# Key copies of units 8 to 23: from VectorE and GpSimd copies to DMAs within SBUF

## The chip, the cores and the metric

The kernel runs on one core of a Trainium2 chip. The metric is the device time of one execution in microseconds (us). Names used below: PE is TensorE, DVE is VectorE, POOL is GpSimd, ACT is ScalarE, SP is SyncE, whose queue issues every DMA of this kernel. SBUF is the on-chip working memory, PSUM the memory that PE writes.

## The reference, cut to what matters

Three steps, all in float32 to high accuracy:

```python
# 1. banded attention with block summaries: q, k, v are [2, 8 heads, 768, 64], block 32, window 16
k_sum = k.reshape(B, H, nb, block, D).max(axis=3)      # "block maxima", 24 per head
v_sum = v.reshape(B, H, nb, block, D).mean(axis=3)
scores_all = concat([where(|i - j| < 16, scale * q @ k.T, -1e9), scale * q @ k_sum.T + log(32)])
attn = softmax(scores_all) @ concat([v, v_sum])
# 2. gated projection on x = attn as [1536, 512]; w_a, w_b are [512, 1536], w_out [1536, 512]
x = ((x @ w_a) * (x @ w_b)) @ w_out
# 3. second layer; w_in is [512, 2048], w_out [2048, 512]
h = x @ w_in;  out = (h - tanh(h)) @ w_out
```

## The kernel before, in words

**Attention in units.** The 2 x 768 positions are cut into 24 units of 64 positions. A unit sees at most 96 neighbouring keys (KW) and the 24 block maxima of its batch (NB), 120 columns in all (NK). The keys of a batch are transposed by PE and evacuated into one buffer `kt` (`prep_k`, L223 to L227): 768 columns of keys, then 24 of block maxima. `kt` has one buffer, so batch 1 (units 12 to 23) overwrites batch 0 (units 0 to 11) once all readers of batch 0 are done. For each unit, `W` (L281 to L289) copies the unit's 96 key columns and, where the buffer does not hold them yet, the 24 maxima from `kt` into a buffer of its own: units 8 to 11 have four of their own (tag "w"), units 12 to 23 take turns in two ("kw"). Then follow the scores (`T2m`, L295), the masked maximum (L306, DVE), the exponential (L310, ACT), the scaling (L324, ACT), a transpose (`T3`, L331) with its evacuation (L334), and the product with the values (`T4`, L344). T4's result x is kept as a rounded part (L351, ACT) and a residue (L352, DVE), since PE multiplies in a shorter format and each product is done as three: high x high, high x low, low x high.

**Blocks.** Eight units make a block of 512 positions. Units 0 to 7 run in the head, in an order written out by hand (`SEQ`, operations L614 to L771); their residues are L726. The units of the next block are spread between the projections of the block at hand.

**Projections.** Position after position PE runs `pos_a` (12 matmuls into PSUM bank "pa", L374), `pos_b` ("pb", L374) and, one group later, `pos_o` (12 matmuls, L402). a0, b0, o0 are those of the first column group, a1, b1 of the second. The result of a is evacuated by ACT (L382, tile ta), multiplied with that of b by DVE (L390, tile tg), and split again (L367 ACT, L368 DVE). The second layer follows with `pos_h` and `pos_o2` (L426, L463).

**Weights.** They come as 64-bit floats, in pieces of 512 KB (L141, L143, tiles stage, x21a, x21b). Piece 0 is for a0, 1 for b0, 2 for a1, 3 for b1, 4 for o0, and so on. A piece is decoded with two ACT steps (L154, L155), a clamp on POOL (L179) and three DVE steps (L161, L164, L165), and split by ACT (L184) and DVE or POOL (L185) into one of four buffers "wsp". Pieces 0 to 2 are done within `SEQ` (L750 to L771).

**What sets the order.** The head follows the order of the code on every engine. Behind it, up to position 72, SP's queue follows the order of the code while a scheduler with its own estimates orders PE, DVE, ACT and POOL; from position 72 on the order of the code holds everywhere. `W` is planned at its unit's place (L564, L565) and for units 8 to 11 in the head (L791, L792).

Of the kernel before, what the change touches and what calls it, by code (L numbers as in the profile page):

```python
# [16 lines left out]
ALU = mybir.AluOpType  # L17
# [22 lines left out]
def band_attention_moe_kernel(ctx: ExitStack, tc: tile.TileContext, q, k, v, w_a, w_b, w_out, w_in, w_out2, out):  # L40
    nc = tc.nc
    mm = nc.tensor.matmul

    B, H, S, D = q.shape
    NT, DM = out.shape
    BLK, WIN = 32, 16
    NB = S // BLK
# [7 lines left out]
    KW = 96  # L55
    NK = KW + NB
# [133 lines left out]
    kt, knat, qn, vst, qb, at_x, X = {}, {}, {}, {}, {}, {}, {}  # L190
# [7 lines left out]
    def kw_of(u):  # L198
        if 8 <= u < 12:
            if u not in kwx:  # L200
                kwx[u] = st([128, NP, NK], "w", 3 * F1)
            return kwx[u]
        return kwb[u % 4 if u < 8 else u % 2]
# [5 lines left out]
    def where(u):  # L209
        b, w = divmod(u, S // 64)  # L210
        return b, w, min(max(w * 64 - WIN, 0), S - KW)
# [37 lines left out]
    def load_q(m):  # L249
        b, w, _ = where(2 * m)  # L250
        t = st([128, H, D], "w", 3 * F1) if m < 8 else st([128, H, D], "qn", 3)
        nc.sync.dma_start(t, q[b, :, w * 64 : w * 64 + 128, :].rearrange("h p d -> p h d"))
        qn[m] = t

    def load_v(u):
        b, w, k0 = where(u)
        t = vw_of(u)
        nc.sync.dma_start(t[0:KW], v[b, :, k0 : k0 + KW, :].rearrange("h p d -> p h d"))
# [19 lines left out]
        for r in range(2):  # L278
            qb[2 * m + r] = qt[:, r]

    def W(u, eng):  # L281
        b, w, k0 = where(u)
        kw = kw_of(u)
        if eng is nc.gpsimd:
            eng.tensor_scalar(kw[:, :, 0:KW], kt[b][:, :, k0 : k0 + KW], 1.0, 0.0, op0=ALU.mult, op1=ALU.add)
        else:
            eng.tensor_copy(kw[:, :, 0:KW], kt[b][:, :, k0 : k0 + KW])
        if u < 4 or 8 <= u < 14:
            nc.vector.tensor_copy(kw[:, :, KW:NK], kt[b][:, :, S : S + NB])  # L289

    def T2m(u, tag):
        qt, kw = qb.pop(u), kw_of(u)
# [231 lines left out]
    def plan(j, fn, *args):  # L524
        at.setdefault(j, []).append((fn, args))
# [29 lines left out]
    for n, u in enumerate(range(8, 24)):  # L555
        j = (n - 8) * 4 + begin[1] + OFF if n >= 8 else n * (begin[1] // 8) + OFF
        b, w, _ = where(u)
        if u % 2 == 0:
            m = u // 2
            if m + 2 < 12:  # L560
                plan(j, load_q, m + 2)
            plan(j, T1, m, "pt", qbd)
            if u >= 12:
                plan(j, W, u, nc.vector)  # L564
                plan(j, W, u + 1, nc.vector)  # L565
        if u % 8 == 0:
            plan(j, new_x, u // 8)
        plan(j + 2, T2, u, "ps")
        plan(j + 3, T2b, u)
        plan(j + 5, T3, u, "pt")  # L570
        plan(j + 7, T4, u, "ps")
        if u + 3 < 24:
            plan(j + 7, load_v, u + 3)
            if 12 <= u + 3 < 15:
                plan(max(j + 7, VM + NC + 5), load_vm, u + 3)
# [6 lines left out]
    def run_plan(j):  # L582
        for fn, args in at.pop(j, ()):
            if fn in (T1, T2, T2b, T3, T4, W, prep_k) and HP:
                with tc.high_priority(offset=HP):
                    fn(*args)
            else:
                fn(*args)
# [199 lines left out]
    with tc.manual_schedule(engines=set(ET_HEAD)):  # L788
        load_q(4)
        load_v(8)  # L790
        for u in range(8, 12):  # L791
            W(u, nc.gpsimd if u % 2 else nc.vector)  # L792
        load_v(9)
        load_v(10)
        for j in range(-12, 0):
            run_plan(j)
# [41 lines left out]
```

## Time and profile before

| | us |
|---|---|
| median of three runs | 667.14 (666.83 to 668.13) |
| profiled execution | 668.39 |
| its span, first to last instruction | 666.6 |
| PE busy in the span | 645.6 |
| DVE busy | 509.3 |
| ACT busy | 471.9 |
| POOL busy | 208.1 |

The profile is of one execution. Its own time is 1.25 us above the median and 1.8 us above its span; differences worked out from its rows are differences of the span. An engine's busy time is the sum of its instructions, and the granted clock tells which share of full speed PE had: 1.00 is 2.4 GHz, 0.50 is 1.2 GHz.

### The profile page before, as it was taken

What the parts mean: (1) busy time and instruction counts of PE and PEld (TensorE: products, weight loads), DVE (VectorE), ACT (ScalarE), POOL (GpSimd) and SP (SyncE); (2) the same over time, 40 slices, a digit from 0 to 9 for tenths busy, and PEclk for the clock granted to TensorE, in tenths of its full rate; (3) what the DMA queues carried; (4) which work ended last, traced back from release to release, by engine and by line L of the source; (5) the groups of instructions that cost most, each with busy time, mean ns of one, the idle gap of its engine ahead of it and who ended that gap; (6) DMA issues with size and microseconds to landing.
All of it is one profiled execution on the core that took longest, in us unless ns stands there. A gap on an engine that the chain in (4) does not pass through costs nothing.

```text
span 666.6 us, 9629 instructions
## 1 busy us (share of the span) xinstructions
PE 645.6 (97%) x3240; PEld 520.3 (78%) x3240; DVE 509.3 (76%) x1019; ACT 471.9 (71%) x1002; POOL 208.1 (31%) x223
## 2 busy tenths in 40 slices
PE   7869999999899999999999999999999999999997
PEld 5658776888688888888888888888888888888885
DVE  5899998999766678637877748777777777777775
ACT  3878888788776778645655548777777777777774
POOL 5771122122001111000111134454444454444441
PEclk8989999999999999999999999999999999999999
DMA  9996996464415435413444200000010000010001
GB/s 205 246 204 202 214 225 184 152 187 132 129 55 168 151 107 167 131 48 111 142 143 142 80 1 0 1 0 1 0 64 1 0 1 0 24 40 1 1 0 63
DMA packets 84781, 62.11 MB, mean 93 GB/s; under 512 B 51892, under 2 KB 75444, under 8 KB 84732
## 3 DMA queue, kind: packets, MB, share of 16 engines
q1 hardware_dynamic: 84732, 61.50, 33.3%
q8 instruction: 25, 0.41, 0.2%
q14 instruction: 24, 0.20, 0.1%
HBM read 54.00 MB, written 7.34 MB: 92 GB/s over the span
## 4 chain that ended last, share of the span: by engine, by line
PE 84%; DVE 7%; ACT 3%; DMA 3%; issue 1%; SPq 1%; POOL 0%; DVEq 0%; ACTq 0%
PE acc L463 20%; PE pa L374 18%; PE pb L374 17%; PE acc L402 13%; PE pt L374 5%; PE ps L374 5%; PE ps L295 2%; PE ps L344 1%; PE pt L331 1%; DVE w L164 1%; PE pt L240 1%; DVE w L165 1%; DMA x20a<-in_q_dram 1%; SPq L614 1%; DMA w<-in_k_dram 1%
## 5 line engine op out<-in xcount | busy, mean ns | idle before, releaser
L185 POOL TENSOR_TENSOR wsp<-w,wsp 128x512 fp32r<-128x512 f32 x97 | 127.4, 1332 | 143.8 <-ACT wsp L184 143.8
L184 ACT ACTIVATE wsp<-w 128x512 fp32r<-128x512 f32 x201 | 121.3, 622 | 19.8 <-PE acc L402 10.1
L185 DVE TENSOR_TENSOR wsp<-w,wsp 128x512 fp32r<-128x512 f32 x104 | 74.7, 719 | 41.7 <-ACT wsp L184 41.5
L179 POOL TENSOR_SCALAR w<-w 128x512 f32<-128x512 f32 x52 | 39.5, 763 | 192.8 <-ACT w L154 184.0
L402 PE MATMUL acc<-gh,wsp 128*128 128x512 f32 x288 | 98.1, 400 | 0.0
L374 PE MATMUL pa<-XA,wsp 128*128 128x512 f32 x336 | 84.9, 399 | 4.6 <-DVE XA L726 4.6
L374 PE MATMUL pb<-XA,wsp 128*128 128x512 f32 x336 | 83.8, 395 | 0.9 <-ACT wsp L768 0.5
L463 PE MATMUL acc<-wsp,gh 128*128 128x512 f32 x256 | 80.5, 396 | 0.0
L374 PEld LDWEIGHTS pa<-XA,wsp 128*128 128x128 f32 x336 | 64.0, 191 | 18.7 <-ACT x21a L155 4.7
L374 PEld LDWEIGHTS pb<-XA,wsp 128*128 128x128 f32 x336 | 62.4, 189 | 15.2 <-ACT wsp L768 1.0
L367 ACT ACTIVATE gh<-tg 128x512 fp32r<-128x512 f32 x68 | 42.3, 622 | 30.6 <-DVE tg L390 30.2
L374 PE MATMUL pa<-XB,wsp 128*128 128x512 f32 x240 | 62.0, 402 | 1.4 <-ACT XB L351 1.4
L402 PEld LDWEIGHTS acc<-gh,wsp 128*128 128x128 f32 x288 | 53.4, 188 | 11.8
L374 PE MATMUL pb<-XB,wsp 128*128 128x512 f32 x240 | 60.0, 394 | 0.0
L402 PE MATMUL acc<-gl,wsp 128*128 128x512 f32 x144 | 56.9, 398 | 0.1
L463 PEld LDWEIGHTS acc<-wsp,gh 128*128 128x128 f32 x256 | 48.2, 188 | 11.1
L368 DVE TENSOR_TENSOR gl<-tg,gh 128x512 fp32r<-128x512 f32 x68 | 47.0, 691 | 9.4 <-ACT gh L367 9.3
L374 PEld LDWEIGHTS pa<-XB,wsp 128*128 128x128 f32 x240 | 45.2, 192 | 11.1 <-ACT XB L351 1.6
L374 PEld LDWEIGHTS pb<-XB,wsp 128*128 128x128 f32 x240 | 44.6, 188 | 9.7
L463 PE MATMUL acc<-wsp,gl 128*128 128x512 f32 x128 | 50.4, 394 | 0.0
L463 PE MATMUL acc<-wsp,vw 128*128 128x512 f32 x192 | 46.5, 390 | 0.0
L463 PEld LDWEIGHTS acc<-wsp,vw 128*128 128x128 f32 x192 | 35.9, 188 | 8.1 <-DVE vw L368 0.4
(305 smaller groups left out, 1184.0 us busy)
## 6 DMA issues: line engine op xcount, KB each, us to landing
stage<-in_moe_w_out_dram SPq DMA_DIRECT2D x19, 512.0 KB, 3.4
stage<-in_moe_w_in_dram SPq DMA_DIRECT2D x16, 512.0 KB, 5.2
stage<-in_moe_w_a_dram SPq DMA_DIRECT2D x8, 512.0 KB, 4.5
w<-wsc SPq DMA_DIRECT2D x16, 256.0 KB, 3.5
vw<-in_v_dram SPq DMA_DIRECT2D x19, 192.0 KB, 3.0
stage<-in_moe_w_b_dram SPq DMA_DIRECT2D x7, 512.0 KB, 5.0
wsc<-x21a SPq DMA_DIRECT2D x8, 256.0 KB, 4.8
wsc<-x21b SPq DMA_DIRECT2D x8, 256.0 KB, 5.9
```

The source lines that it names most:

```text
L164: nc.vector.scalar_tensor_tensor(r, t[:, :, 1], -0x40000000, r, op0=ALU.bitwise_and, op1=ALU.bitwise_or)
L165: nc.vector.tensor_tensor(r, r, t[:, :, 0], op=ALU.add)
L179: nc.gpsimd.tensor_scalar(rf, rf, HI_HI, HI_LO, op0=ALU.min, op1=ALU.max)
L184: nc.scalar.activation(s[:, 0, :], r, AF.Copy)
L185: eng.tensor_tensor(s[:, 1, :], r, s[:, 0, :].bitcast(F32), op=ALU.subtract)
L240: mm(pp, mavg[:, NB - 4 - 4 * c : 2 * NB - 4 - 4 * c], vch.pop(c).rearrange("p h d -> p (h d)"), start=(c == 0), stop=(c == NC - 1),)
L295: mm(pp[:, p, 0:NK], qt[:, p, :], kw[:, p, :], start=True, stop=True)
L367: nc.scalar.activation(dst[0], src, AF.Copy)
L368: eng.tensor_tensor(dst[1], src, dst[0].bitcast(F32), op=ALU.subtract)
L374: mm(dst, w, xx, start=(kk == 0 and n == 0), stop=(kk == KC - 1 and n == 2))
L402: mm(acc[blk][d][:, c0:c1], w, t, start=(f == 0 and c0 == 0 and n == 0), stop=(f == F1 - 1 and n == 2))
L463: mm(a[c], g[:, cs], s[:, i, :], start=(f == 0 and n == 0), stop=(f == F2 - 1 and n == 2))
```

## The change

`W` no longer takes an engine. The 96 key columns are copied by one DMA on SP's queue, and where the maxima are needed a second DMA copies 24 columns. The condition for the maxima is written as u < 14; `W` is called for units 8 to 23, so they are the same six units as before. Units 0 to 7 keep their copies in `SEQ`. There are 16 + 6 = 22 new DMAs in place of 14 DVE and 2 POOL copies of keys and 6 DVE copies of maxima. Lines of the changed kernel behind `W` have numbers lower by two; this text and the prediction name them by the numbers of before.

```diff
--- before.py
+++ after.py
@@ -278,15 +278,13 @@
         for r in range(2):
             qb[2 * m + r] = qt[:, r]
 
-    def W(u, eng):
+
+    def W(u):
         b, w, k0 = where(u)
         kw = kw_of(u)
-        if eng is nc.gpsimd:
-            eng.tensor_scalar(kw[:, :, 0:KW], kt[b][:, :, k0 : k0 + KW], 1.0, 0.0, op0=ALU.mult, op1=ALU.add)
-        else:
-            eng.tensor_copy(kw[:, :, 0:KW], kt[b][:, :, k0 : k0 + KW])
-        if u < 4 or 8 <= u < 14:
-            nc.vector.tensor_copy(kw[:, :, KW:NK], kt[b][:, :, S : S + NB])
+        nc.sync.dma_start(kw[:, :, 0:KW], kt[b][:, :, k0 : k0 + KW])
+        if u < 14:
+            nc.sync.dma_start(kw[:, :, KW:NK], kt[b][:, :, S : S + NB])
 
     def T2m(u, tag):
         qt, kw = qb.pop(u), kw_of(u)
@@ -561,8 +559,8 @@
                 plan(j, load_q, m + 2)
             plan(j, T1, m, "pt", qbd)
             if u >= 12:
-                plan(j, W, u, nc.vector)
-                plan(j, W, u + 1, nc.vector)
+                plan(j, W, u)
+                plan(j, W, u + 1)
         if u % 8 == 0:
             plan(j, new_x, u // 8)
         plan(j + 2, T2, u, "ps")
@@ -789,7 +787,7 @@
         load_q(4)
         load_v(8)
         for u in range(8, 12):
-            W(u, nc.gpsimd if u % 2 else nc.vector)
+            W(u)
         load_v(9)
         load_v(10)
         for j in range(-12, 0):
```

Three places where the order moves. First DVE, end of the head. Here XA is x of the first block, and `XA<-pa`, `XA<-pb` are the residues L726 of the two units computed last (1 and 3). Before:

```order
L726 TENSOR_TENSOR XA<-pt,XA 128x4x64
L287 COPY w<-kt 128x4x96
L289 COPY w<-kt 128x4x24 x2
L287 COPY w<-kt 128x4x96
L289 COPY w<-kt 128x4x24 x2
L726 TENSOR_TENSOR XA<-pa,XA 128x4x64
L759 TENSOR_SCALAR w<-w 128x512
L761 SCALAR_TENSOR_TENSOR w<-stage,w 128x512
L726 TENSOR_TENSOR XA<-pb,XA 128x4x64
```

In the changed kernel:

```order
L724 TENSOR_TENSOR XA<-pt,XA 128x4x64
L724 TENSOR_TENSOR XA<-pa,XA 128x4x64
L757 TENSOR_SCALAR w<-w 128x512
L759 SCALAR_TENSOR_TENSOR w<-stage,w 128x512
L724 TENSOR_TENSOR XA<-pb,XA 128x4x64
```

The six copies are gone, and the residue from "pa" stands directly behind the one from "pt".

A little later on DVE, in the changed kernel: the residue split of piece 2 (wsp), then the product for b0, and only then the three steps of decoding for piece 3 (x21a):

```order
L769 TENSOR_TENSOR wsp<-w,wsp 128x512
L388 TENSOR_TENSOR tg<-pb,ta 128x512
L277 COPY qbd<-pt 64x8x64
L161 TENSOR_SCALAR w<-w 128x512
L164 SCALAR_TENSOR_TENSOR w<-x21a,w 128x512
L366 TENSOR_TENSOR gl<-tg,gh 128x512
L165 ISA w<-x21a,w 128x1024
L161 TENSOR_SCALAR w<-w 128x512
```

Before, the decoding of piece 3 stood ahead of the product for b0. ACT shows the same. Here `x21a` is the load of piece 3, `x21b` of piece 4, and `ta<-pa` the evacuation of a0. Before:

```order
L768 ACTIVATE wsp<-w 128x512
L724 ACTIVATE XA<-pb 128x4x64
L752 ACTIVATE stage<-stage 128x512 x2
L154 ACTIVATE w<-x21a 128x512
L155 ACTIVATE x21a<-x21a 128x512
L768 ACTIVATE wsp<-w 128x512
L275 ACTIVATE qbd<-pt 64x8x64
L154 ACTIVATE w<-x21b 128x512
```

In the changed kernel:

```order
L766 ACTIVATE wsp<-w 128x512
L722 ACTIVATE XA<-pb 128x4x64
L750 ACTIVATE stage<-stage 128x512 x2
L766 ACTIVATE wsp<-w 128x512 x2
L155 ACTIVATE stage<-stage 128x512
L380 ACTIVATE ta<-pa 128x512
L154 ACTIVATE w<-x21a 128x512
L155 ACTIVATE x21a<-x21a 128x512
L275 ACTIVATE qbd<-pt 64x8x64
L154 ACTIVATE w<-x21b 128x512
L155 ACTIVATE x21b<-x21b 128x512
L155 ACTIVATE stage<-stage 128x512
```

The first step for piece 3 has moved from ahead of the evacuation of a0 to behind it.

Second SP, at the end of the head. The first row loads piece 5; `w<-kt` are the new copies of keys (96 columns) and maxima (24). Before:

```order
L141 DMA stage<-in_moe_w_a_dram 128x4x256
L258 DMA vw<-in_v_dram 96x8x64 x2
L214 DMA w<-in_k_dram 128x8x64
L252 DMA w<-in_q_dram 128x8x64
L141 DMA stage<-in_moe_w_b_dram 128x4x256
```

In the changed kernel:

```order
L141 DMA stage<-in_moe_w_a_dram 128x4x256
L285 DMA w<-kt 128x4x96
L287 DMA w<-kt 128x4x24
L285 DMA w<-kt 128x4x96
L141 DMA stage<-in_moe_w_b_dram 128x4x256
L287 DMA w<-kt 128x4x24
L285 DMA w<-kt 128x4x96
L143 DMA stage<-in_moe_w_out_dram 128x1024
L287 DMA w<-kt 128x4x24
L285 DMA w<-kt 128x4x96
L287 DMA w<-kt 128x4x24
L258 DMA vw<-in_v_dram 96x8x64 x2
```

The loads of pieces 6 and 7 (w_b and w_out) now stand among the copies, and the loads of v, k and q behind them.

Third PE, at the end of the first block. XB is x of the second block; `pt<-ident,qn` are the transposes of q for unit 16, `ps<-at,vw` is T4 of unit 15, `ps<-kw` the scores of units 16 and 17. Before:

```order
L402 MATMUL acc_886<-gl,wsp 128x512
L402 MATMUL acc_886<-gh,wsp 128x512
L269 MATMUL pt<-ident,qn 128x128 x4
L344 MATMUL ps<-at,vw 64x64 x8
L374 MATMUL pa<-XB,wsp 128x512
L374 MATMUL pb<-XB,wsp 128x512
L295 MATMUL ps<-kw,qbd 128x120 x4
L374 MATMUL pa<-XB,wsp 128x512 x11
L374 MATMUL pb<-XB,wsp 128x512 x11
```

In the changed kernel:

```order
L400 MATMUL acc_886<-gh,wsp 128x512
L329 MATMUL pt<-ident,e 120x128 x4
L342 MATMUL ps<-at,vw 64x64 x8
L269 MATMUL pt<-ident,qn 128x128 x4
L372 MATMUL pa<-XB,wsp 128x512
L372 MATMUL pb<-XB,wsp 128x512
L372 MATMUL pa<-XB,wsp 128x512 x11
L372 MATMUL pb<-XB,wsp 128x512 x11
L293 MATMUL ps<-kw,qbd 128x120 x4
```

Before, eight L402 stood between the transposes of unit 15 (L331) and these rows; they now stand ahead of those transposes. The transposes of q have moved behind T4, and the scores of unit 16 from ahead of the long run on "pa" to behind that on "pb".

## Rows read from the trace of the kernel before

**Rows 1.** The page's busy times: engine, us, share of the span, instructions.

```profile
PE 645.6 (97%) x3240; PEld 520.3 (78%) x3240; DVE 509.3 (76%) x1019; ACT 471.9 (71%) x1002; POOL 208.1 (31%) x223
```

**Rows 2.** Stretches of the span: us; busy us and instructions per engine; granted clock; DMA share; GB/s.

```profile
44.00:48.00 4.00, 3.45 (x9) 2.38 (x10) 3.79 (x8) 1.91 (x4) 1.31 (x2) 0.50 1.37 210
48.00:60.00 12.00, 12.00 (x55) 9.88 (x55) 11.53 (x28) 9.88 (x26) 2.53 (x4) 0.90 0.74 212
60.00:80.00 20.00, 19.61 (x115) 15.90 (x114) 18.49 (x41) 16.90 (x41) 3.82 (x5) 1.00 0.78 202
80.00:100.00 20.00, 19.46 (x110) 15.74 (x109) 19.50 (x42) 16.31 (x39) 5.53 (x7) 1.00 1.00 229
...
300.00:400.00 100.00, 100.00 (x438) 81.88 (x437) 72.47 (x113) 55.52 (x98) 16.53 (x19) 1.00 0.30 103
```

**Rows 3.** Chain of waits, 34 to 66 us: start, us, engine, tile, line.

```profile
41.81 1.79 DVE w L289 x2
```

**Rows 4.** Order of time on DVE, 36 to 62 us: start, us, line, operation, tiles.

```profile
39.95 0.41 DVE L726 TENSOR_TENSOR XA<-pt,XA 128x256 fp32r<-128x256 f32 x1
40.29 0.40 DVE L287 COPY w<-kt 128x384 f32<-128x384 f32 x1
40.61 0.62 DVE L289 COPY w<-kt 128x96 f32<-128x96 f32 x2
41.15 0.66 DVE L287 COPY w<-kt 128x384 f32<-128x384 f32 x1
41.73 1.87 DVE L289 COPY w<-kt 128x96 f32<-128x96 f32 x2
43.53 0.41 DVE L726 TENSOR_TENSOR XA<-pa,XA 128x256 fp32r<-128x256 f32 x1
...
45.38 0.68 DVE L763 CUSTOM_DVE_ANT_0 w<-stage,w 128x1024 uint16<-128x1024 uint16 x1
```

**Rows 5.** Order of time on PE, 30 to 95 us; in brackets the wait ahead.

```profile
44.08 0.77 PE L374 MATMUL pa<-XA,wsp 128*128 128x512 f32 x1 [4.58 <-DVE XA L726]
...
47.79 3.68 PE L374 MATMUL pa<-XA,wsp 128*128 128x512 f32 x10
...
57.69 2.88 PE L374 MATMUL pb<-XA,wsp 128*128 128x512 f32 x12
```

**Rows 6.** Order of time on ScalarE, 36 to 62 us.

```profile
42.42 0.65 ACT L154 ACTIVATE w<-x21a 128x512 f32<-128x512 f32 x1
```

**Rows 7.** Groups of instructions: count, busy us, mean ns, idle before.

```profile
L390 DVE TENSOR_TENSOR tg<-pb,ta 128x512 f32<-128x512 f32 x36 | 24.6, 684 | 10.1 <-PE pb L374 9.8
...
L306 DVE CUSTOM_DVE_ANT_0 e<-ps,mask 128x120 f32<-128x120 f32 x64 | 14.1, 274 | 5.2 <-PE ps L295 5.2
```

**Rows 8.** DMA issues: tiles, queue, count, KB each, median us to landing.

```profile
vw<-in_v_dram SPq DMA_DIRECT2D x19, 192.0 KB, 3.0
...
w<-in_q_dram SPq DMA_DIRECT2D x4, 256.0 KB, 6.0
```

**Rows 9.** Half-microsecond stretches with 1 KB pieces, then with 256-byte pieces on the queue.

```profile
42.50:43.00 0.50, 0.00 (x0) 0.00 (x0) 0.50 (x1) 0.50 (x3) 0.50 (x1) 1.00 1.06 369
...
45.00:45.50 0.50, 0.50 (x4) 0.30 (x2) 0.50 (x3) 0.00 (x0) 0.00 (x0) 0.50 1.40 197
```

**Rows 10.** Order of time on SP's queue, 0 to 320 us.

```profile
40.50 0.37 SPq L141 DMA_DIRECT2D stage<-in_moe_w_a_dram  x1
...
141.83 0.33 SPq L258 DMA_DIRECT2D vw<-in_v_dram  x1
```

**Rows 11.** Order of time on PE, 95 to 160 us: scores of unit 14.

```profile
150.68 1.05 PE L295 MATMUL ps<-kw,qbd 128*128 128x120 f32 x8
```

**Rows 12.** Chain of waits, 165 to 190 us.

```profile
171.76 4.08 DMA stage<-in_moe_w_in_dram
```

**Rows 13.** Order of time on PE, 160 to 230 us: the second block's first matmul.

```profile
178.34 0.50 PE L374 MATMUL pa<-XB,wsp 128*128 128x512 f32 x1 [1.43 <-ACT XB L351]
```

## The prediction

> **What bounds the kernel now.** I read the page's busy times first. TensorE (PE) is busy for 645.6 of 666.6 us [rows 1], so the kernel can gain at most the 21 us in which PE rests, plus what PE loses at a low clock. The table by stretches shows where that is: from 300 to 400 us PE runs 438 matmuls in 100 us, 0.23 us each, with nothing left over, while from 44 to 48 us the granted clock is 0.50, the 1.2 GHz level, and from 48 to 60 us still 0.90 in the mean [rows 2]. So PE bounds nearly everything, and the open stretch is the change from the head (attention of units 0 to 7) to the first projection, about 39.5 to 60 us. The chain of waits goes through VectorE (DVE) there: 1.79 us of it is the copy of the block maxima [rows 3]. The order of time on DVE shows why. Between the residue of one unit, which ends at 40.36, and that of the next, which starts at 43.53, stand two copies of keys and four of block maxima for units 8 to 11 [rows 4]. PE's first projection matmul waits 4.58 us for exactly that residue (XA by L726): it needs the PSUM bank "pa", which the residue still reads [rows 5]. After 60 us PE is full, and DVE too: 18.49 and 19.50 of 20 us busy in the two stretches to 100 us [rows 2]. DVE's finishing times matter that long, later they have slack.
>
> **The copies in the head.** DVE loses six copies that fill 40.29 to 43.53, 3.24 us [rows 4]. The order shows the residue for "pa" directly behind the one for "pt". So the residues, the last decoding steps of pieces 1 and 2 and the start of projection a0 all move forward by 3.24 us; GpSimd, which loses two key copies, is no later. The ten matmuls of a0 that ran from 47.79 [rows 5] can start at 47.79 - 3.24 = 44.55.
>
> What is late next is weight piece 3, for projection b1. Before, ScalarE took up its first step at 42.42 [rows 6]. In the changed order that step stands behind the evacuation of a0, and DVE's three steps for it stand behind the product for b0 (L390), which needs b0 finished on PE. At full clock a0's ten end at 44.55 + 2.3 = 46.85 and b0's ten, next in PE's order, at 49.15. Then DVE has before the residue split of piece 3: L390, L277, three decoding steps, L368, L161, four score maxima, L164 and the split. By the 0.68 of a 512-wide step, 0.42 of a shift (as the short residue) and 4 x 0.27 for the maxima [rows 4, 7] that is 7 x 0.68 + 2 x 0.42 + 1.1 = 6.7, less some 0.5 by which records overlap: 6.2 us. The split ends at 55.35, and b1's third matmul, the first that reads it, starts near 55.5. Before, b1 began at 57.69 [rows 5] and its third matmul came 0.47 later, 58.2. That is 2.7 us earlier, less 0.4 for four key transposes that PE had done by then and now does later: **+2.3 us** as the upper bound.
>
> The lower bound is the clock. Before, half clock lasted to about 50.4 (0.10 below full over 12 us is 2.4 us at half [rows 2]). If it lasts as long now, 44.55 to 50.4 at half speed costs 2.9 us: b0 ends at 52.05, b1's third matmul starts at 58.4, and the term is -0.6 us. PE rests less ahead of a0 than before (two short waits in place of one of 4.58 us), but it is still little used from 39.5 to 44. I expect half clock for about half of those 5.85 us, which costs 1.45 us and leaves 2.3 - 1.45, and take **+0.9 us**. That DVE stays full to 100 us, and so may take back some of what PE is ahead, is a reason not to take more.
>
> **The new DMAs.** 22 DMAs are added on SP's queue: 16 of keys (196,608 bytes in 512 pieces of 384 bytes) and 6 of maxima (49,152 bytes in 512 pieces of 96). No row shows this form from SBUF to SBUF. The nearest are v loads of 192 KB, which land 3.0 us after issue in the median, and q loads of 256 KB in a full queue, 6.0 [rows 8]; I take those as both ends for one copy, and 3 to 4 once the queue is short. For the queue's own time the row of the 1 KB pieces moves 369 GB/s and that of the 256-byte pieces 197 GB/s [rows 9]. 197 GB/s is 770 pieces per us, so 512 pieces hold the queue 0.67 us; by bytes alone a key copy would be 0.53. I take 0.67 for each DMA.
> In the head SP issues the load of piece 5 at 40.50 [rows 10], then three key copies and two of maxima mixed with the loads of pieces 6 and 7. Piece 7 then lands near 40.9 + 1.4 + 5 x 0.67 + 2 x 1.4 + 1.5 = 50 (1.4 is 512 KB at 369 GB/s, 1.5 what remains of a landing). ScalarE comes to it only behind work that ends near 51 to 52, so the loads are covered, with 1 to 2 us to spare: **0**, if the price per DMA holds.
> From unit 12 on the copies are issued behind a v load that waits for PE's output matmuls of an earlier unit. For unit 14: v load at 141.83 [rows 10], one weight load, one q load and two key copies at about 0.5 us each, so the second is out at 144 and lands at 147 to 150, against 150.68 for the scores in the old order [rows 11]. The cover is 0.7 to 3.7 us, so **0**. What is queued behind on SP are weight loads and stores for the last layer; they go out 1 us later, and the engine that waits for them is ScalarE.
>
> The Trainium skill, "DMA: Bandwidth & Descriptors", Specifications, says that transfers under 512 bytes are slower since the DMA engine reads and writes back. By it every added piece would cost more than the row of the 256-byte loads. The same page, "Why small descriptors are slow (HBM only)", says that SBUF to SBUF does not suffer from small pieces; by that 0.53 would do. The trace agrees that 256-byte pieces from HBM move at about half the rate [rows 9]; it holds no pieces of this size within SBUF.
>
> **DVE from 57 us on.** Ten of the twelve later key copies, at 0.40 us or less [rows 4], lie where PE is full; freeing them is worth nothing beyond the cover it gives to the first two.
>
> **The block boundary.** At 178.34 the second block's first matmul waited 1.43 us, and ScalarE got there late because it had waited for a weight load of 4.08 us [rows 12, 13]. The scheduler reorders PE there: the block's L402 now all stand ahead of the transposes of unit 15, which leaves T4 of that unit without cover (about 1.5 us more waiting), but the transposes of q now cover the wait behind T4, and the scores of unit 16 come one pair of projections later. I bound this by -1.5 and +2.0 us (the wait of 1.43 gone and little clock lost) and take **+0.5**: one pair's worth of work (0.23 x 2) in place of the wait.
>
> **Sum.** 0.9 + 0 + 0 + 0.5 = 1.4 us less. The profiled execution took 668.39 us (666.6 of span and 1.8 around it), which gives 667.0; it is 1.25 above the median of 667.14. The measured median should go to 667.14 - 1.4 = **665.7 us**.
>
> **Rivals.**
> Given back (no change): the order that keeps piece 3 behind b0 and the half clock use up the whole start. For it: DVE idles some 3 us for b0 in the new order and has almost no room until 100 us [rows 2]. Against it: the split of piece 3 still comes out earlier by the sum at full clock. Time: 667.14 with the -0.6 to +0.6 of that term, 666.5 to 667.7.
> Slow small copies (slower): if one DMA of 512 small pieces holds the queue 2.0 us, not 0.67, the five ahead of piece 7 take 10 us, it lands at 56.6 (50 + 5 x 1.33), ScalarE holds the split of piece 3 until then, and b1 begins 4.8 us later than forecast: 4.8 - 1.4 = 3.4 us slower, 670.5. It eats the gain from about 1.35 us per DMA on (1.8 us of slack and 1.4 of gain, over five). For it: nothing of this form is in the trace, and 256-byte pieces are already at half rate [rows 9]; against it: 192 KB in 768 pieces land in 3.0 us in all [rows 8]. The skill's rule on transfers under 512 bytes would point this way.
> Clock stays up (more): the shorter rests ahead of a0 leave PE at 2.4 GHz, the first term is +2.3 and the boundary gains its 2.0: 662.8.
>
> **How the numbers follow.** Forecast 0.48 (its own range 664 to 667), given back 0.27, slow copies 0.14, clock stays up 0.11. About 0.2%, 1.33 us, can be told from no change here. The forecast case lies beyond that in 0.39 of its 0.48 (a stall shorter than reckoned adds to it more easily than a longer one takes), the clock case fully: faster 0.50. Given back and the rest of the forecast, less 0.04 for a new wait that no row points to: same 0.32; slower 0.18. The range runs from the clock case to the start of the slow case: 662.5 to 668.6.
>
> **What would show it.** Right: PE's first projection matmul near 40.9 and a0's ten near 44.6; a wait of PE in b1 for a split by L185 near 53 to 55.5; the key copies landing within 3 to 4 us and no wait of PE's score matmuls on a DMA. Wrong: a0 still at 44 (the copies were not the cause); ScalarE waiting over 2 us for pieces 6 or 7 (slow copies); half clock past 50 us, which takes the first term; or PE waiting in scores of units 12 to 23 for kw.

## The result and the profile after

The changed kernel takes 671.43 us (median of 4 runs, 670.69 to 673.34), against 667.14 before: ratio 1.0064 [1.0051, 1.0078]. It is slower by 4.3 us where 1.4 us less were forecast. Its profiled execution took 671.29 us with a span of 669.6, which is 3.0 more than the span of before; the rest of the 4.3 lies in the profiled execution of before, 1.25 above its median.

The page's busy times (engine, us, share, instructions) answer to [rows 1]:

```profile
PE 646.5 (97%) x3240; PEld 520.9 (78%) x3240; DVE 501.8 (75%) x999; ACT 473.1 (71%) x1002; POOL 206.1 (31%) x221
```

VectorE lost 20 instructions and 7.5 us, and the span still grew. The stretches answer to [rows 2] (us; busy us and instructions of PE, weight loads, DVE, ACT and POOL; granted clock; DMA share; GB/s):

```profile
44.00:48.00 4.00, 4.00 (x11) 3.15 (x10) 2.58 (x3) 1.21 (x2) 1.46 (x1) 0.50 1.04 258
48.00:60.00 12.00, 9.48 (x41) 7.48 (x40) 8.42 (x23) 9.56 (x24) 2.28 (x3) 0.93 0.84 199
60.00:80.00 20.00, 20.00 (x112) 16.48 (x112) 18.61 (x40) 15.87 (x37) 4.51 (x6) 0.96 0.78 209
80.00:100.00 20.00, 19.01 (x109) 15.22 (x108) 18.58 (x40) 17.95 (x43) 5.96 (x8) 1.00 1.09 256
...
300.00:400.00 100.00, 100.00 (x439) 81.93 (x438) 71.38 (x111) 54.23 (x96) 16.52 (x19) 1.00 0.32 103
```

From 48 to 60 us TensorE now rests for 2.5 of 12 us where it was full before, and the clock is below full again from 60 to 80. From 300 us on TensorE is full at full clock in both. TensorE's rows (order of time; the wait in brackets) answer to [rows 5, 13]; L711 is the last T4 of the head, L400 the first output product:

```profile
38.05 0.67 PE L711 MATMUL pb<-gh,w 120*64 120x64 f32 x16
40.66 0.49 PE L372 MATMUL pa<-XA,wsp 128*128 128x512 f32 x1 [1.95 <-DVE w L757]
42.73 0.79 PE L372 MATMUL pa<-XA,wsp 128*128 128x512 f32 x1 [1.58 <-DVE XA L724]
...
45.03 3.87 PE L372 MATMUL pa<-XA,wsp 128*128 128x512 f32 x10
48.74 2.43 PE L372 MATMUL pb<-XA,wsp 128*128 128x512 f32 x10
...
55.80 0.73 PE L372 MATMUL pb<-XA,wsp 128*128 128x512 f32 x2 [1.03 <-ACT wsp L184]
58.03 4.14 PE L372 MATMUL pb<-XA,wsp 128*128 128x512 f32 x10 [1.49 <-DVE wsp L185]
...
62.36 0.48 PE L400 MATMUL acc<-gh,wsp 128*128 128x512 f32 x1
...
181.00 1.01 PE L342 MATMUL ps<-at,vw 120*64 120x64 f32 x16 [2.00 <-ACT at L332]
```

The same two points in the kernel before:

```profile
38.84 0.67 PE L713 MATMUL pb<-gh,w 120*64 120x64 f32 x16
...
60.41 0.39 PE L402 MATMUL acc<-gh,wsp 128*128 128x512 f32 x1
```

The first projection matmul came at 40.66, 3.42 us earlier than before. But 0.79 us of that stood already at the last T4 of the head, ahead of the place where the copies had been, and is not the change's: in the fourteen profiles of this document that T4 starts anywhere from 37.98 us (late_p3_behind) to 39.30 (late_copies), and neither of these two has a new transfer. Then b1 waited twice, 2.52 us together, for its own weights (piece 3), and its last ten took 4.14 us, against 2.43 for b0's ten at full clock, since the clock had fallen a second time. The first output product came at 62.36, 1.95 us later than before; counted from the last T4 of the head it is 2.74 us later. ScalarE and VectorE show why b1's weights were late; they answer to [rows 6] and [rows 4]:

```profile
48.94 0.60 ACT L380 ACTIVATE ta<-pa 128x512 f32<-128x512 f32 x1 [1.66 <-PE pa L372]
49.43 0.66 ACT L154 ACTIVATE w<-x21a 128x512 f32<-128x512 f32 x1
```

```profile
51.27 0.69 DVE L388 TENSOR_TENSOR tg<-pb,ta 128x512 f32<-128x512 f32 x1 [3.86 <-PE pb L372]
...
54.40 0.69 DVE L165 CUSTOM_DVE_ANT_0 w<-x21a,w 128x1024 uint16<-128x1024 uint16 x1
...
56.88 1.10 DVE L185 TENSOR_TENSOR wsp<-w,wsp 128x512 fp32r<-128x512 f32 x1
```

ScalarE took up piece 3 at 49.43, not at 42.42, behind an evacuation that itself waited for TensorE; VectorE idled 3.86 us for b0's product with piece 3's steps queued behind it. The copies themselves, as transfers (tiles, queue, count, KB, median us to landing; answer to [rows 8]):

```profile
kw<-kt SPq DMA_DIRECT2D x12, 192.0 KB, 4.2
...
w<-kt SPq DMA_DIRECT2D x4, 192.0 KB, 4.3
w<-kt SPq DMA_DIRECT2D x4, 48.0 KB, 4.4
```

They land some 4 us after issue in the median, and no row of TensorE waits for one of them.

For all kernels below I use one measure of where time goes: from a table of half-microsecond stretches, TensorE's resting time plus its busy time times (1 - granted clock), added up over the head, the middle of block 0, and the boundaries of blocks 1 and 2. It comes from the one profiled execution of each, and so is rough: a_late_head and tail_on_top have the same order in the head, and yet the granted clock from 40 to 50 us is 0.83 in one profile and 0.66 in the other, and the head columns are 5.8 and 6.8. Differences of about 1 us in a column may be the execution and not the kernel. The ratios rest on all runs; the kernels ran beside runs of the kernel before, on several chips.

| kernel | ratio to before [95%] | 36-62 us | 62-176 us | 176-302 us |
|---|---|---|---|---|
| before | 1 | 8.1 | 1.0 | 3.6 |
| changed | 1.0064 [1.0051, 1.0078] | 10.6 | 2.3 | 3.7 |
| head_dma | 1.0040 [1.0028, 1.0053] | 9.8 | 2.4 | 2.1 |
| tail_dma | 1.0009 [0.9995, 1.0023] | 8.1 | 1.5 | 2.2 |
| dma_on_top | 1.0031 [1.0018, 1.0044] | 8.8 | 2.4 | 2.2 |
| p3_early | 1.0070 [1.0048, 1.0091] | 7.6 | 2.2 | 5.3 |
| p34_head_dma | 1.0047 [1.0029, 1.0065] | 6.9 | 4.1 | 3.7 |
| p34_after | 1.0031 [1.0019, 1.0043] | 6.0 | 4.8 | 1.7 |
| late_copies | 0.9997 [0.9983, 1.0010] | 5.2 | 2.2 | 1.5 |
| a_late | 1.0037 [1.0022, 1.0051] | 6.2 | 2.5 | 2.1 |
| a_late_head | 1.0003 [0.9992, 1.0014] | 5.8 | 3.2 | 1.1 |
| tail_pool | 0.9995 [0.9984, 1.0006] | 5.9 | 1.6 | 2.3 |
| tail_on_top | 0.9975 [0.9963, 0.9987] | 6.8 | 3.2 | 1.3 |
| late_p3_behind | 0.9960 [0.9944, 0.9975] | 7.8 | 1.3 | 0.2 |

By this measure the changed kernel loses 2.5 us more than before in the head, 1.3 from 62 to 176 us and 0.1 at the boundaries. The first matmul of block 2 tells the same in time: it starts at 298.73 for 295.69, 3.04 us later, and this lag stays to the end. Of it 1.95 stood at the first output product; the other 1.1 arose between there and block 2.

### The profile page after: what moved, and what is told of

The parts are those of the page before. It is cut to its first block, busy times and chain, and to the rows that moved or that the text cites. A ratio compares the mean times of both kernels' runs of the same rounds, so it can differ in the third digit from the quotient of the medians.

```text
span 669.6 us, 9637 instructions
## 1 busy us (share of the span) xinstructions
PE 646.5 (97%) x3240; PEld 520.9 (78%) x3240; DVE 501.8 (75%) x999; ACT 473.1 (71%) x1002; POOL 206.1 (31%) x221
## 4 chain that ended last, share of the span: by engine, by line
PE 80%; DVE 8%; DMA 5%; ACT 3%; issue 1%; SPq 1%; POOL 0%; DVEq 0%
PE acc L461 20%; PE pa L372 17%; PE pb L372 17%; PE acc L400 12%; PE pt L372 5%; PE ps L372 5%; PE ps L293 1%; DMA w<-in_k_dram 1%; DVE w L164 1%; DVE w L165 1%; PE ps L342 1%; DMA stage<-in_moe_w_in_dram 1%; DMA x21b<-in_moe_w_a_dram 1%; PE pt L240 1%; DMA x20a<-in_q_dram 1%
## 5 line engine op out<-in xcount | busy, mean ns | idle before, releaser
L400 PE MATMUL acc<-gh,wsp 128*128 128x512 f32 x288 | 98.2, 400 | 1.1 <-ACT wsp L184 1.1
L372 PE MATMUL pb<-XA,wsp 128*128 128x512 f32 x336 | 85.5, 401 | 3.3 <-DVE wsp L185 2.2
L400 PEld LDWEIGHTS acc<-gh,wsp 128*128 128x128 f32 x288 | 53.7, 188 | 13.5 <-ACT wsp L184 1.7
L400 PE MATMUL acc<-gl,wsp 128*128 128x512 f32 x144 | 56.9, 398 | 0.0
```

The costliest lines, as they stand in the source:

```text
L372: mm(dst, w, xx, start=(kk == 0 and n == 0), stop=(kk == KC - 1 and n == 2))
L400: mm(acc[blk][d][:, c0:c1], w, t, start=(f == 0 and c0 == 0 and n == 0), stop=(f == F1 - 1 and n == 2))
```

## The experiments

Theory T: the loss is in the order of the instructions, above all in the place of piece 3's decode. Theory D: the transfers cost it. Theory L: the later units cost it. The code hands its operations to the scheduler in numbered plan slots: slot j is emitted just ahead of position j of the projections, and the slots below 0 at the end of the head, where the order on SP, ACT, DVE and POOL is still fixed. Diffs show only the lines that matter.

**One half of the change at a time.** head_dma:

```diff
         kw = kw_of(u)
+        if u < 12:
+            nc.sync.dma_start(kw[:, :, 0:KW], kt[b][:, :, k0 : k0 + KW])
+            if u < 14:
+                nc.sync.dma_start(kw[:, :, KW:NK], kt[b][:, :, S : S + NB])
+            return
```

> Units 8 to 11 by DMA as in the changed kernel, units 12 to 23 copied on VectorE as before. Theory T (the loss is in the order of the instructions: with the six head copies gone, ScalarE takes piece 3's decode behind a0's evacuation and VectorE takes it behind b0's product, so TensorE waits for b1's weights and its clock falls a second time): the first o product of block 0 starts near 62.4 us as in the changed kernel (60.4 before), the total is 668.5 to 670.5. Theory D (the transfers cost the time, about 4.3 us for 22 of them): 8 of 22 are left, so about 668.7 and nothing is bound to the wait for b1's weights. Theory L (the 14 later transfers and the order behind 60 us cost it): 666.5 to 667.8.

670.41 us (before, beside it, 667.86). The head is that of the changed kernel:

```profile
57.28 4.63 PE L379 MATMUL pb<-XA,wsp 128*128 128x512 f32 x10 [1.49 <-DVE wsp L185]
62.42 0.78 PE L407 MATMUL acc<-gh,wsp 128*128 128x512 f32 x1
```

tail_dma has the same lines under `if u >= 12:`.

> Units 8 to 11 copied by VectorE and GpSimd as before, units 12 to 23 by DMA. Theory T: head as before, the first o product at 60.4 +- 0.3 us, and the total 667.1 to 668.5 (what the changed order behind 60 us costs, up to 1.3). Theory D: 14 of 22 transfers, so about 669.8. Theory L: 669 to 671.5.

668.17 us, not told from before; its first output product is at 60.5. So the head's half alone carries 2.6 us (670.41 - 667.86) and the later units' half alone 0.3; the other 1.4 of the 4.3 stands in neither half alone (tail_dma's interval reaches to 1.5). L falls as the main cause. D, which gives every transfer the same price, misses both times: 668.7 for 670.41 and 669.8 for 668.17. T stands, and so does a D in which only the head's transfers cost time.

**The transfers without the removal of the copies.** dma_on_top:

```diff
+        nc.sync.dma_start(scr[u][:, :, 0:KW], kt[b][:, :, k0 : k0 + KW])
+        if u < 14:
+            nc.sync.dma_start(scr[u][:, :, KW:NK], kt[b][:, :, S : S + NB])
```

> The kernel before with all its copies on VectorE and GpSimd, and besides them the same 22 transfers from the key tiles, into DRAM scratch that nothing reads. The order on the engines stays that of before up to about 44 us and piece 3's decode stays ahead of b0's product. Theory T: the transfers themselves cost nothing, first o product 60.4 +- 0.7 us, total 666.5 to 668.7 (the spread that a changed order behind 50 us brings). Theory D: 670 to 672. Theory L: 669 to 672.

669.76 us: above T's range, just below D's, within L's. The first output product came at 60.7, 0.3 us later than before, and 0.9 later counted from the last T4 of the head; the clock does not fall a second time. So in the head the eight transfers, with what else changed there, cost 0.3 to 0.9 us. From 62 to 176 us, where the order differs again from that of before, it loses 1.4 us more. This run does not tell T from D.

**The decode of piece 3 earlier.** p3_early, with all 22 transfers:

```diff
-            ja = first[u] - DL
+            ja = first[u] - DL if i > 3 else -12
```

> The changed kernel, with all 22 transfers, but with the decode of piece 3 (b1's weights) emitted at plan slot -12 and not -2, so that ScalarE has it ahead of a0's evacuation and VectorE begins it ahead of b0's product. Theory T: b1's last ten begin by 55.5 us without a wait for its weights, the clock stays at full speed behind 51 us, the first o product is at 58.5 to 60.0 us (62.36 in the changed kernel), and the total is 667.5 to 669.5, so 2 to 4 below the changed kernel's 671.43. Theories D and L: the transfers are all there, so it stays at 670.5 to 672.5.

672.03 us: as D said, while the head did about what T said. b1 no longer waits, the head's loss falls from 10.6 to 7.6, and the wait has moved on to o0's weights, piece 4, and to the start of block 2:

```profile
59.96 0.50 PE L400 MATMUL acc<-gh,wsp 128*128 128x512 f32 x1 [1.72 <-ACT wsp L184]
...
297.89 0.69 PE L342 MATMUL ps<-at,vw 120*64 120x64 f32 x16 [1.09 <-ACT at L332]
299.06 0.50 PE L372 MATMUL pa<-XA,wsp 128*128 128x512 f32 x1 [0.48 <-ACT XA L349]
```

In the changed kernel neither wait of block 2's start exists. The scheduler had put unit 23's last transpose behind the last output products. T's total fell, T's head held. With pieces 3 and 4 early (`i > 4`), first with the later units on VectorE (p34_head_dma), then on the changed kernel (p34_after):

> Units 8 to 11 by DMA, units 12 to 23 copied on VectorE as before, and the decodes of pieces 3 and 4 (b1's and o0's weights) both emitted at plan slot -12. With piece 3 alone TensorE waited 1.72 us for o0's weights, at 59.96 us. Theory T: neither b1 nor o0 waits for its weights, the first o product starts at 58.0 to 59.5 us, the total is 665.0 to 667.0. Theory G: the wait goes on to the next piece, first o product 60 to 61 us, total 667 to 669. Theory D (the transfers cost 0.2 us each): 668 to 670.

> The changed kernel with all 22 transfers and the decodes of pieces 3 and 4 emitted at plan slot -12. Theory T: first o product at 58.0 to 59.5 us; behind it the order of units 12 to 23 is again another one, with the 0 to 3.5 us that such orders cost so far, so 666 to 669. Theory D: 670 to 672.

670.85 us with the later units on VectorE, beyond every range, and 669.25 for the other, between T's range and D's. The first output products are at 58.5 and 58.0, as T said; the next pieces are late instead (p34_head_dma):

```profile
62.88 0.73 PE L379 MATMUL pa<-XA,wsp 128*128 128x512 f32 x2 [0.92 <-ACT wsp L184]
63.89 2.57 PE L379 MATMUL pa<-XA,wsp 128*128 128x512 f32 x10 [0.28 <-DVE wsp L185]
...
77.63 2.56 PE L379 MATMUL pa<-XA,wsp 128*128 128x512 f32 x10 [1.08 <-DVE wsp L185]
```

**The copies out of the way, no transfer.** late_copies is the kernel before with its loop over W(8) to W(11) moved behind the loop over the plan slots below 0:

```diff
-        for u in range(8, 12):
-            W(u, nc.gpsimd if u % 2 else nc.vector)
         load_v(9)
         load_v(10)
         for j in range(-12, 0):
             run_plan(j)
+        for u in range(8, 12):
+            W(u, nc.gpsimd if u % 2 else nc.vector)
```

> The kernel before, without any transfer in place of a copy: the eight head copies stay on VectorE and GpSimd but are emitted behind the plan slots below 0, so that VectorE has XA's last residues and piece 3's decode (b1's weights) ahead of them. Theory T (what counts is that the copies leave the place ahead of XA's last residue while piece 3's decode stays ahead of b0's product): a0's last ten start near 45.0 us as in the changed kernel, b1's last ten by 56 us without a second fall of the clock, the first o product at 58.5 to 59.8 us (before 60.41, changed 62.36), total 665.0 to 666.8. Theory G (the head to the first o product is bounded by the decode of five pieces, whatever VectorE does first): first o product 60 to 61 us, total 666.5 to 668.5.

666.87 us, not told from before (667.14 beside it): G's range, at the edge of T's. The head itself is better than either said, 2.9 us less lost than before (5.2 for 8.1) and the first output product at 57.85; 1.2 us are given back by 176 us.

**The same place for the transfers.** a_late is the changed kernel with the same move; a_late_head has it with units 12 to 23 on VectorE.

> The changed kernel with all 22 transfers; only the place changes at which the eight head transfers are emitted: behind the plan slots below 0 instead of ahead of them, in the same region of fixed order. ScalarE then has piece 3's decode ahead of a0's evacuation again (as before), and VectorE begins it ahead of b0's product. Theory T (the head's loss is the place of that decode, not the transfers): no second fall of the clock at 58 us, the first o product at 57.5 to 59.0 us (62.36 in the changed kernel, 57.85 with the late copies); behind it what the order gives back, 0 to 3 us, so 666 to 669.5. Theory D (the transfers cost 0.2 us each, 4.3 together): first o product 61 to 63 us, total 670 to 672.

> As a_late for units 8 to 11 (transfers, emitted behind the plan slots below 0), with units 12 to 23 copied on VectorE as in the kernel before. Theory T: first o product at 57.5 to 59.0 us and a total of 664.5 to 667.5. Theory D: 668 to 670. Theory P (what the head gains is paid back behind it, since TensorE then waits for the pieces that come next): first o product at 57.5 to 59.0 us, waits of 2 to 3 us between 60 and 80 us as with pieces 3 and 4 early, total 667 to 670.

669.03 and 667.12 us, in T's ranges (the second also at the lower end of P's). These are the clearest pairs: all transfers stay, eight of them are only emitted elsewhere, and the ratio goes from 1.0064 to 1.0037 against the changed kernel and from 1.0040 to 1.0003 against head_dma, 1.8 and 2.5 us with before taken as 667.1. The intervals of the first pair just touch, those of the second lie apart. a_late's profile is of the shortest of its nine executions (667.23). ScalarE and TensorE of a_late:

```profile
41.68 0.65 ACT L154 ACTIVATE w<-x21a 128x512 f32<-128x512 f32 x1
...
47.66 0.60 ACT L380 ACTIVATE ta<-pa 128x512 f32<-128x512 f32 x1
```

```profile
56.12 0.40 PE L400 MATMUL acc<-gh,wsp 128*128 128x512 f32 x1
...
60.58 0.74 PE L372 MATMUL pa<-XA,wsp 128*128 128x512 f32 x2 [0.62 <-ACT wsp L184]
62.62 2.57 PE L372 MATMUL pa<-XA,wsp 128*128 128x512 f32 x10 [0.87 <-DVE wsp L185]
```

Piece 3 is taken up at 41.68, ahead of a0's evacuation, and the first output product stands at 56.12, 6.2 us ahead of the changed kernel, about 1 of it because unit 8's scores now come behind it. D's 61 to 63 is out. The second fall of the clock is gone: of the fourteen profiles only those of the changed kernel and head_dma show a granted clock below 1.00 between 54 and 70 us. As theory P said, part goes at once, in waits for the next pieces.

**The later units.** tail_pool is a_late with units 12 to 23 copied by GpSimd; tail_on_top is a_late_head with 14 transfers to scratch beside VectorE's copies.

> As a_late, but the 14 copies of units 12 to 23 are done by GpSimd and not by transfers; the order of ScalarE and VectorE is that of a_late until well behind 80 us, since VectorE has none of these copies in either. What is asked is why the later units by transfer cost 1.6 to 1.9 us more than by VectorE. Theory O (the order of the instructions that comes when VectorE's copies go, and not the transfers): total as a_late, 668.3 to 669.7. Theory D (the transfers): total as with copies on VectorE, 666.5 to 667.8.

> The version with late head transfers and units 12 to 23 copied on VectorE (667.12), and besides the copies the same 14 transfers into DRAM scratch that nothing reads; the order of ScalarE and VectorE is that of this version until well behind 80 us. Theory O: total 666.5 to 667.8, transfers cost nothing beside the copies. Theory D: 668.5 to 669.5.

667.28 and 665.42 us. The first is in D's range (1.75 less than a_late when the transfers go), the second below both ranges (1.7 less than a_late_head when the same number of transfers is added); by the ratios it is 2.8 and 1.9. No row of TensorE in a_late waits for a transfer of these units. If the transfers themselves cost time, the second should have been slower, so the order that comes with each edit is the likelier cause; but the transfers to scratch carry nothing that is needed, so this is argued and not shown, and which part of the order it would be stays open.

**The reverse.** late_p3_behind, no transfers, has piece 3's decode emitted last ahead of slot 0 and outside the region of fixed order:

```diff
-        plan(ja, dec_a, u)
-        plan(ja + 1, dec_b_next, i)
+        plan(ja if i > 3 else 'end', dec_a, u)
+        plan(ja + 1 if i > 3 else 'end', dec_b_next, i)
...
+    run_plan('end')
     reg = ExitStack()
```

> The reverse test, without a single transfer: the version with the late copies (666.87; first o product at 57.85 us), but with the decode of piece 3 emitted last of all ahead of slot 0 and outside the region of fixed order, so that its last steps on VectorE come behind b0's product and unit 8's scores, as in the changed kernel. Theory T: TensorE waits for b1's weights again, the clock falls a second time behind 50 us, the first o product is at 61.5 to 64 us, and the total 668.5 to 671.5. Theory D (the loss belongs to the transfers): no transfers, so 666.5 to 667.8 and the first o product at 57.5 to 59 us.

664.24 us, the fastest of all and below both ranges. b1 waited, as T said, but once, and the clock held; ScalarE's first step had stayed ahead of a0's evacuation (45.99 for 49.03), so this was half the test that I meant. The scheduler had also put eight output products, 57.69 to 59.60, between b1's first two matmuls and its last ten, where the changed kernel waited 1.49 us. Then the boundary at 176 us lost nearly nothing (last row; the kernel before follows it):

```profile
57.11 0.73 PE L374 MATMUL pb<-XA,wsp 128*128 128x512 f32 x2 [1.31 <-ACT wsp L184]
```

```profile
57.00:62.00 5.00, 4.89 (x21) 3.91 (x22) 5.00 (x12) 5.00 (x13) 0.48 (x1) 1.00 0.89 253
176.00:186.00 10.00, 9.82 (x47) 8.20 (x48) 6.92 (x20) 7.46 (x20) 0.61 (x1) 1.00 0.67 193
```

```profile
176.00:186.00 10.00, 8.13 (x46) 6.36 (x45) 3.92 (x15) 5.08 (x17) 0.00 (x0) 0.83 0.70 203
```

So T in its strong form, that the place of this decode sets the total, has fallen. What is left of it is below.

## Why the prediction was wrong

**The copies in the head (forecast +0.9, bounds -0.6 and +2.3; measured -1.95 at the first output product, -2.74 counted from the last T4 of the head).** This step failed, at three places, here counted from that T4. The largest is a cost that the step left out: behind the waits for piece 3 the clock fell, and b1's ten matmuls took 4.14 us, against 2.43 for b0's ten. These 1.7 us stood in neither bound. The text listed the wait as a sign that it was right and gave it no price; among the signs that it was wrong it had half clock past 50 us, which came here as a second fall.

The second place is the start. The copies' 3.24 us were taken over whole, but a0's ten moved forward by 1.97 us only; that they began at 45.03, near the forecast 44.55, is partly luck, the 0.79 us that the profile was ahead. The residue from "pa" did move by 3.25. What took back 1.26 are the two decoding steps behind it, before and then in the changed kernel:

```profile
43.86 0.54 DVE L759 TENSOR_SCALAR w<-w 128x512 int32<-128x512 int32 x1
44.43 0.69 DVE L761 SCALAR_TENSOR_TENSOR w<-stage,w 128x512 int32<-128x512 int32 x1
```

```profile
39.82 0.83 DVE L757 TENSOR_SCALAR w<-w 128x512 int32<-128x512 int32 x1
40.69 1.66 DVE L759 SCALAR_TENSOR_TENSOR w<-stage,w 128x512 int32<-128x512 int32 x1
```

Before, it was the second pair of maxima copies that had been slow, 1.87 us for 0.62 of the first pair [rows 4]. Both slow stretches lie beside a residue split on GpSimd (40.42 to 41.79, before 42.26 to 43.54); that this is the reason is not shown. The third place is VectorE's work from b0's product to the split of piece 3, 6.7 us for the 6.2 of the sum.

The rest of the step came true: ScalarE and VectorE in the order that the text read out, and the half clock of a0's ten, which ended near 48 us and cost some 1.4 us, as forecast (with luck: a_late_head and tail_on_top show that its length varies between executions). b1's third matmul came at 58.03, inside the bound of 58.4, but only by the 0.79 us of lead.

That the place of the transfers in the code brought the second fall is shown by two pairs: with the same transfers emitted behind the plan slots, the decode stands ahead, the second fall is gone (in the one profile of each), and 1.8 and 2.5 us of the total come back. That the scheduler kept the decode behind because the eight transfers stood ahead of it in the region of fixed order is my reading of these orders, not shown by itself. And a better order would not have brought the forecast gain either: late_copies, with a head that loses 2.9 us less than before and no transfer, has the time of before (0.9997).

**The new transfers (forecast 0).** Right as far as the rows show: 0.59 to 0.73 us each on the queue for the 0.67 taken, 3.6 to 4.4 us to landing (medians of the groups), no wait of TensorE on one, and none of ScalarE on a load of piece 6 or 7. That they cost nothing in the total is not shown: dma_on_top, which only adds them, is 0.31% slower, its order changed as well. The Trainium skill ("DMA: Bandwidth & Descriptors") has two rules that bear on them, that transfers under 512 bytes are slowed (Specifications) and that copies from SBUF to SBUF are spared the price of small pieces ("Why small descriptors are slow (HBM only)"). No run here tells them apart, since none copies within SBUF in pieces of 512 bytes or more. The 256-byte loads of [rows 9], which the prediction took for the cheaper side of the first rule, lie under 512 bytes too. The slow rival has its sign and nearly its size (671.4 for 670.5) by chance: its sign, ScalarE waiting over 2 us for piece 6 or 7, did not come.

**VectorE from 57 us on (forecast 0).** Too kind. From 62 to 176 us the changed kernel loses 2.3 for 1.0 us. Of the ten other kernels with an altered head order, eight lose 1.1 to 3.7 us more there than before did; the order of before was good in this stretch. The step took an order change as free wherever no row of before waited.

**The boundary (forecast +0.5).** Measured -0.1: 2.00 us of wait for T4 without cover, in place of 1.43 and 0.44, the same half clock behind it (0.83 in the mean from 176 to 186 us in both). The text named that wait as its lower case.

**Why repairs of the head did not simply pay.** Ahead of 62 us ScalarE and VectorE decode and split a piece for each run of 12 matmuls; when one piece is early, TensorE waits for the next (p3_early for o0, p34 at 62.88 and 77.63, a_late at 60.58). Beyond that, each edit re-orders units 12 to 23 as well, and the total moved by some 2 us either way with no cause that I could show. Part of it may be the clock at the boundary: from 176 to 186 us it is 0.83 in the profiles of before, the changed kernel, p3_early and p34_head_dma, 0.96 in p34_after and 1.00 in the other nine, and 0.83 over 10 us is 1.7 us. The clock also differs between executions of one kernel: beside head_dma, before took 665.71 us at a mean granted clock of 0.995 and 669.05 at 0.987. Open are therefore the part of the loss behind 62 us (1.1 to 1.3 us in the profile) and why p3_early, whose head is repaired, is no faster than the changed kernel beyond the waits at block 2.

A version that beats both exists: late_p3_behind, 0.4% faster than before, without transfers. With transfers it is tail_on_top, 0.25%; its scratch transfers do nothing useful, so it shows only that the order can be had.

## What to carry to other kernels

When a scheduler orders the program, removing work from one engine is an edit of the order of all; look first for what now stands behind a result that the busiest engine has yet to make. Price a forecast wait of TensorE with a worse case: the wait, and the matmuls behind it at half clock (here 2.5 and 1.7 us). Before blaming a new kind of transfer, keep it and move only the place where it is emitted. And before reading a lead off two profiles, compare a point ahead of the change.

## What the runs showed of the hardware

Bytes hardly matter for these copies within SBUF, at 512 pieces each: in the head of the changed kernel 48 KB in pieces of 96 bytes landed 4.4 us after issue, 192 KB in pieces of 384 bytes 4.3 (medians of four), and each held the queue for 0.59 to 0.73 us.

The length of a wait alone does not tell whether the clock falls. From 57 to 62 us, first in the changed kernel (a wait of 1.03 us ended at 55.80, one of 1.49 at 58.03), then in p3_early (one of 1.72, ended at 59.96):

```profile
57.00:62.00 5.00, 3.97 (x10) 3.11 (x11) 4.14 (x8) 3.70 (x13) 1.18 (x2) 0.66 0.93 261
```

```profile
57.00:62.00 5.00, 3.04 (x15) 2.12 (x14) 4.23 (x10) 4.15 (x11) 0.30 (x1) 1.00 0.89 192
```

p3_early had the longer single wait and kept 2.4 GHz, up to 80 us too; the changed kernel, with two waits and two matmuls between them, fell to 1.2. At the boundary of block 1 it is the same. Before, waits of 1.43 and 0.44 us stood beside a mean clock of 0.83 from 176 to 186 us; in a_late_head one of 2.17 us left it at 1.00:

```profile
177.06 0.69 PE L349 MATMUL ps<-at,vw 120*64 120x64 f32 x16 [2.17 <-ACT at L339]
```

```profile
176.00:186.00 10.00, 8.94 (x58) 7.50 (x59) 3.61 (x13) 5.22 (x10) 0.62 (x1) 1.00 0.71 203
```

What decides it is not shown here.
